# Moving one chunk's gate broadcast, two first states and four loads inside a fused mLSTM and MoE kernel

## The chip, the cores and the metric

The kernel runs on one core of a Trainium2 chip. The metric is the device time of one execution in microseconds (us). Three runs of the kernel before gave 401.60, 401.11 and 400.73 us, a median of 401.11 us. The execution whose trace is read here took 400.72 us; its instructions span 398.9 us, and 1.8 us lie around them. Durations come from that one execution, so a forecast is made as its 400.72 us plus or minus what the change does, and then set beside the median, which lies 0.39 us higher.

## The reference

Two stages are fused. The first is an mLSTM recurrence over 768 steps for 2 batches and 8 heads of width 40, with stabilised forget and input gates, an outer-product state, a normaliser and an output gate. The second is a mixture of four experts, each token weighted by given probabilities:

```python
C = f_stab[:, :, None, None] * C + i_stab[:, :, None, None] * np.einsum('bhd,bhe->bhde', vt, kt)
n = f_stab[:, :, None] * n + i_stab[:, :, None] * kt
y[:, :, t] = o * h_tilde / denom                      # denom = max(|n . q|, 1)
...
for e in range(E):
    h = np.maximum(x @ w1[e], 0.0)                    # 320 -> 1024
    out += p[:, e:e + 1] * (h @ w2[e])                # 1024 -> 320
```

## The kernel before, in words

The order of the work is written out by hand: every engine (TensorE or PE, VectorE or DVE, ScalarE or ACT, GpSimd or POOL) and SP's queue of transfers carries out its instructions in the order in which the program issues them. The recurrence is cut into 12 chunks of 128 steps; chunk n belongs to batch n % 2 and to place n // 2 in the sequence. Pairs of chunks share their loads (index j = n // 2).

What is done for a chunk:

- `load_qk(j)`, `load_vk(j)`, `load_o(j)` (L401 to L412) bring q and k, v and k, and the output gates. `load_o(j)` writes into two slices of the result tile `acc`; `gate_o(j)` (L414) turns them into sigmoids in place, on ACT.
- `spread(n)` (L421) copies a chunk's forget gates over all partitions with eight matmuls into two PSUM banks; this is done for chunks 0 to 3. From chunk 4 on, `load_f(n)` (L432) reads the same gates, broadcast, back from the scratch tensor `f_d`, 512 KB for each chunk. Chunk 4's go into a part of `acc` that is not used yet.
- `decay(n)` (L441) makes the decay matrix from them, in two scans on DVE; `scores(n)` (L470) is q times k on PE, `weigh(n)` (L478) multiplies the two on DVE.
- `values(n)` (L452) and `keys(n)` (L463) scale v and k on POOL. `state(n)` (L484) is the chunk's outer product on PE, added on DVE to what `carry(n)` (L506, POOL) scaled. For the first two chunks nothing is carried, and ACT copies the product.
- `inter(n)` (L515) reads the carried state on PE and scales it on ACT (`yb`), `intra(n)` (L534) does the part inside the chunk on PE, `norm(n)` (L543) adds the two, multiplies by the output gate and divides, on DVE (L551 to L558).
- `turn(n)` (L560) transposes the normalised chunk on PE into `px`, ACT copies the high part into `xst`, `turn_lo(n)` (L574) subtracts it on DVE for the low part. The experts' matmuls take both parts.

Gates of the chunks after the first are prepared together: `gate_p` (L326) puts start values into a PSUM bank, `gate_b` (L332) scans over them on DVE, `gate_last` (POOL), `gate_t` and `gate_l` (L348, L373) turn them to the layouts that the chunks want. The first expert's weights are split into a high part on ACT and a low part on POOL: `quarter_hi`, `quarter_lo` for w1, `split_w2` for w2 (L118 to L128).

PSUM has eight banks in four pools of two: `ps_h` (hidden products), `ps_o` (expert outputs, tag `po`), `ps_w` (tag `w`) and `ps_y` (tag `y`). A tile waits for the readers of the tile that had its bank before.

After a prologue written line by line (L581 to L715), a loop runs over chunks 2 to 11. In each it issues state(n), turn_lo(n - 1), inter(n + 1), intra(n), norm(n), scores(n + 1), then values, keys, weigh and carry of chunk n + 1, and then the pieces that `PLAN` (L38) lists for it: H (a hidden bank of the first expert), O (a part of its output), D (the first half of a later decay), T (turn). For chunk 2 the plan is "H03 D O00 T". From about 110 us on only the experts are left, four of them, 512 tokens at a time.

The transfers are all issued by SP. In the order of the program around the change: w1 of the first expert, qk(1), `pw` (the tokens' weights), the scratch write `f_d`, w2 of the first expert (`w2r`, 1,280 KB), vk(1) (640 KB), o(1) (320 KB), qk(2) (832 KB), vk(2) (640 KB), f(4) (512 KB), f(5), f(6), o(2), qk(3), vk(3).

Of the kernel before, what the change touches and what calls it, by code (L numbers as in the profile page):

```python
# [18 lines left out]
L = 128  # L19
# [16 lines left out]
NPE = 4  # L36
# [22 lines left out]
def tile_mlstm_moe(ctx, tc, gt, qk, vk, ot, dp, w1, w2, out):  # L59
# [33 lines left out]
    def copy(eng, dst, src):  # L93
        if eng is nc.scalar:
            eng.activation(dst, src, AF.Copy)
        else:
            eng.tensor_copy(dst, src)
# [147 lines left out]
    with ExitStack() as actx:  # L245
# [80 lines left out]
        def gate_p(c0, c1):  # L326

            n = (c1 - c0) * L
            bps[c0] = ps_w.tile([L, 512], F32, tag="w", name="bp")[0:BH, 0:n]
            nc.scalar.activation(bps[c0], bs[:, c0:c1].rearrange("p c t -> p (c t)"), AF.Copy)  # L330

        def gate_b(c0, c1):  # L332
# [72 lines left out]
        def load_vk(j, c=None):  # L405
            if j not in vks:
                vks[j] = a2.tile([L, 2, 2, H, D], F32, tag="vk", name="vk")
            c = slice(0, 2) if c is None else slice(c, c + 1)
            nc.sync.dma_start(vks[j][:, c], vk[j, :, c])
# [68 lines left out]
        def weigh(n):  # L478
            pms[n] = a1.tile([L, H, L], F32, tag=f"pm{n % 2}", name="pm")
            pm, dd = (t.rearrange("k (p r) t -> k r p t", r=2) for t in (pms[n], dds[n]))  # L480
            for r in range(2):
                nc.vector.tensor_mul(pm[:, r], ss[n][r], dd[:, r])  # L482

        def state(n, pool=ps_w, tag="w"):  # L484

            b, c, vv, kk = n % B, n // B, vvs[n], kp[n % 2]
            if c == NC - 1:
                return
            st = pool.tile([L, NP, L], F32, tag=tag, name="st")
            blocks = [(slice(64 * r, 64 * r + D), slice(DN * r, DN * r + DN)) for r in range(2)]  # L490
            for p in range(NP):
                for r, (q, q2) in enumerate(blocks):
                    h = 2 * p + r
                    nc.tensor.matmul(  # L494
                        st[q, p, q2], kk[:, h], vv[:, h, 0:D + 1], start=True, stop=True
                    )
            cout = cs[b]
            if c == 0:
                for q, q2 in blocks:
                    copy(nc.scalar, cout[q, :, q2], st[q, :, q2])  # L500
            else:
                cd = cds.pop(n)
                for q, q2 in blocks:
                    nc.vector.tensor_add(cout[q, :, q2], cd[q, :, q2], st[q, :, q2])

        def carry(n):  # L506
            b, c = n % B, n // B
# [77 lines left out]
        load_qk(0, 1)  # L585
        load_o(0)
        load_vk(0, 1)
        load_w1(0)
        load_w1(1)
        load_qk(1, 0)  # L590
        load_qk(1, 1)
        nc.sync.dma_start(pw, dp)
        make_identity(nc, ident)
        nc.gpsimd.memset(ib, 0.0)
        lasts[1] = gp.tile([L, B * NP, NC - 1], F32, name="last")
# [36 lines left out]
        for _ in range(3):  # L632
# [5 lines left out]
        gate_starts(1, NC, nc.gpsimd)  # L638
        gate_pair(1, 2, nc.gpsimd)
        values(1, LO)  # L640
        intra(0)
        nc.sync.dma_start(f_d, fs)
        w2r = raws.tile([L, NF, DM], F32, tag="raw", name="w2r")
        nc.sync.dma_start(w2r, w2[0])
        load_vk(1)
        load_o(1)
        load_qk(2)
        load_vk(2)
        load_f(NPE, acc[:, 8:12].rearrange("p c d -> p (c d)")[:, 0:H * L]
               .rearrange("p (h t) -> p h t", h=H))  # L650
        quarter_hi(0)
# [1 line left out]
        quarter_hi(1)  # L653
        norm(0)
        intra(1)
        turn(0)
        spread(2, ps_o, "po")
        norm(1)
        turn_lo(0)
        turn(1)  # L660
        keep_warm(256, ps_w, "w")
        gate_p(1, NC - 1)
        gate_p(NC - 1, NC)
        turn_lo(1)
        quarter_lo(1)
        quarter_hi(2)
        quarter_hi(3)
        keys(0)
        keys(1)
        quarter_lo(2)  # L670
        gate_b(1, NC - 1)
        gate_b(NC - 1, NC)
        gate_last(1, NC)
        quarter_lo(3)
        psum_e = const.tile([L, NCH, 1], F32, name="psum_e")
        nc.gpsimd.tensor_add(psum_e, pw[:, :, 0:1], pw[:, :, 1:2])
        for e in range(2, NE):
            nc.gpsimd.tensor_add(psum_e, psum_e, pw[:, :, e:e + 1])
        nc.gpsimd.tensor_scalar_add(psum_e, psum_e, 1e-9)
        first = work[0]  # L680
        first.products(0)
        turn_d(0, 2)
        nc.scalar.activation(ib[32:32 + BH, g1], gat[:, 0, g1], AF.Copy)
        decay(2)
        first.products(2)
        first.corners(0)
        first.relu(0)
        first.relu(2)
        scores(2)
        state(0, ps_y, "y")  # L690
        state(1, ps_y, "y")
        weigh(2)
        split_w2_hi(w2s, 0, 2, w2r)
        split_w2_hi(w2s, 2, 2, w2r)
        split_w2_lo(w2s, 0, 2, w2r, nc.gpsimd)
        spread(3, ps_o, "po")
        gate_t(1, NC)
        first.products(4)
        gate_l(1, NC)
        decay(3)  # L700
        values(2)
        keys(2)
        carry(2)
        split_w2_hi(w2s, 4, 2, w2r)
        split_w2_lo(w2s, 2, 2, w2r, nc.gpsimd)
        first.corners(4)
        first.relu(4)
        inter(2, ps_o, "po")
        gate_o(1)
        gctx.close()  # L710
        a0 = actx.enter_context(
            tc.tile_pool(name="a0", bufs=1, side="right", reuse_waits="tile")
        )
        load_f(NPE + 1)
        load_f(NPE + 2)  # L715

        def step(a):
            w, k = work[int(a[1])], int(a[2])
            if a[0] == "H":
# [5 lines left out]
        for n in range(2, NCH):  # L725
            j, cc = n // 2, n % 2
            plan = PLAN[n].split()
            nxt = n + 1 < NCH
            if cc == 0 and 2 < j + 1 < NG:
                load_qk(j + 1)  # L730
                load_vk(j + 1)
            if cc == 0:
                if j > 1:
                    gate_o(j)
                if j + 1 < NG:
                    load_o(j + 1)
            if n == NCH - 2:
                raw1 = load_w1e(1)
            state(n)
            if n - 1 in pxs:  # L740
                turn_lo(n - 1)
            if nxt:
                inter(n + 1)
            intra(n)
            norm(n)
            if nxt:
                scores(n + 1)
            for a in plan:
                if a[0] == "H":
                    work[int(a[1])].corners(int(a[2]) // 2 * 4)  # L750
                    break
            if nxt:
                values(n + 1)
                if n == 4:
                    split_w2_lo(w2s, 6, 2, w2r, nc.gpsimd)
                    nc.gpsimd.tensor_mul(pw, pw, psum_e.to_broadcast([L, NCH, NE]))
                if n > 2:
                    decay(n + 1, 1)
                if n > 3 and n + 3 < NCH:
                    load_f(n + 3)  # L760
                keys(n + 1)
                weigh(n + 1)
                carry(n + 1)
            if n == 2:
                split_w2_lo(w2s, 4, 2, w2r, nc.gpsimd)
                nc.vector.reciprocal(psum_e, psum_e)
            for a in plan:
                if a == "T":
                    turn(n, ps_w, "w")
                    turn_d(n, n + 1)  # L770
                elif a == "D":
                    decay(n + 2, 0)
                elif a == "L":
                    turn_lo(n)
                elif a == "S":
                    split_w2_hi(w2s, 6, 2, w2r)
                else:
                    step(a)
# [103 lines left out]
```

## Time and profile before

| | |
|---|---|
| median of three runs | 401.11 us |
| the profiled execution | 400.72 us |
| its span, first to last instruction | 398.9 us |
| PE busy | 393.3 us (99%) |
| DVE busy | 174.4 us (44%) |
| ACT busy | 128.1 us (32%) |
| POOL busy | 77.7 us (19%) |

Start and duration in a timeline are microseconds from the first instruction. "x8" says that eight instructions are merged. The bracket at the end of a line is the engine's idle time ahead of the line and what ended it; a line without one followed its predecessor at once. Matmuls overlap, so that a line of PE can start before the one ahead of it ends; the time that a group really takes is from its start to the next one's start.

### The profile page before, as it was taken

What the parts mean: (1) busy time and instruction counts of PE and PEld (TensorE: products, weight loads), DVE (VectorE), ACT (ScalarE), POOL (GpSimd) and SP (SyncE); (2) the same over time, 40 slices, a digit from 0 to 9 for tenths busy, and PEclk for the clock granted to TensorE, in tenths of its full rate; (3) what the DMA queues carried; (4) which work ended last, traced back from release to release, by engine and by line L of the source; (5) the groups of instructions that cost most, each with busy time, mean ns of one, the idle gap of its engine ahead of it and who ended that gap; (6) DMA issues with size and microseconds to landing.
All of it is one profiled execution on the core that took longest, in us unless ns stands there. A gap on an engine that the chain in (4) does not pass through costs nothing.

```text
span 398.9 us, 7170 instructions
## 1 busy us (share of the span) xinstructions
PE 393.3 (99%) x3054; PEld 357.4 (90%) x3054; DVE 174.4 (44%) x313; ACT 128.1 (32%) x309; POOL 77.7 (19%) x93
## 2 busy tenths in 40 slices
PE   9899999999999999999999999999999999999996
PEld 6799999999988988989989989889889889799896
DVE  8888989798624023133132152141241341331321
ACT  4876354455336332025021051071130320220310
POOL 4894622320007110007100010053000100000000
PEclk9999999999999999999999999999999999999999
DMA  6999529391000203000200031003000001000001
GB/s 159 316 307 283 157 82 250 89 284 83 2 2 12 121 18 139 2 0 19 114 2 0 2 106 52 2 1 133 0 2 0 2 0 49 18 16 35 17 18 49
DMA packets 15000, 29.34 MB, mean 74 GB/s; under 512 B 1000, under 2 KB 10760, under 8 KB 13656
## 3 DMA queue, kind: packets, MB, share of 16 engines
q1 hardware_dynamic: 14968, 28.88, 23.2%
q8 instruction: 24, 0.39, 0.4%
q14 instruction: 8, 0.07, 0.1%
HBM read 26.86 MB, written 2.02 MB: 72 GB/s over the span
## 4 chain that ended last, share of the span: by engine, by line
PE 96%; DMA 2%; DVE 1%; SPq 1%; issue 0%
PE ph L166 43%; PE po L226 43%; PE s L476 3%; PE y L538 2%; DMA qk<-in_qk 2%; PE y L523 2%; PE px L565 1%; PE st L494 1%; PE fb L426 0%; SPq L582 0%; DVE pm L482 0%; PE pit L356 0%; SPq L403 0%; DVE acc L236 0%; DVE xr L555 0%
## 5 line engine op out<-in xcount | busy, mean ns | idle before, releaser
L166 PE MATMUL ph<-xst,w1s 128*128 128x512 f32 (+3 forms) x840 | 174.9, 364 | 0.0
L226 PE MATMUL po<-w2s,h 128*128 128x320 f32 x1152 | 173.0, 309 | 0.0
L226 PEld LDWEIGHTS po<-w2s,h 128*128 128x128 f32 x1152 | 169.9, 188 | 1.2
L166 PEld LDWEIGHTS ph<-xst,w1s 128*128 128x128 f32 (+1 forms) x840 | 140.9, 188 | 28.3 <-issue 4.2
L209 ACT ACTIVATE h<-ph 128x512 fp32r<-128x512 f32 x96 | 57.3, 598 | 194.3 <-PE ph L166 194.3
L210 DVE SCALAR_TENSOR_TENSOR h<-ph,h 128x512 fp32r<-128x512 f32 x96 | 66.2, 690 | 102.1 <-ACT h L209 101.5
L236 DVE SCALAR_TENSOR_TENSOR acc<-po,pw,acc 128x320 f32<-128x320 f32 x36 | 19.8, 551 | 99.9 <-PE po L226 99.9
L109 POOL TENSOR_TENSOR w1s<-raw,w1s 128x512 fp32r<-128x512 f32 (+1 forms) x24 | 23.6, 1023 | 96.6 <-ACT w1s L106 96.6
L109 POOL TENSOR_TENSOR w2s<-raw,w2s 128x640 fp32r<-128x640 f32 x6 | 9.5, 1576 | 98.2 <-ACT w2s L106 98.2
L445 DVE TENSOR_TENSOR_SCAN dd<-fb,id 128x512 f32<-128x512 f32 x22 | 26.7, 1231 | 0.0
L530 ACT ACTIVATE yb<-y,ibT 128x41 f32<-128x41 f32 x80 | 16.0, 322 | 0.8 <-PE y L523 0.8
L166 PE MATMUL ph<-xd,w1s 64*128 64x512 f32 (+1 forms) x56 | 15.9, 392 | 0.0
L482 DVE TENSOR_TENSOR pm<-s,dd 128x512 f32<-128x512 f32 x24 | 15.4, 684 | 1.0
L476 PE MATMUL s<-qk 64*128 64x128 f32 (+1 forms) x192 | 15.2, 284 | 0.6 <-DMA qk<-in_qk 0.6
L476 PEld LDWEIGHTS s<-qk 64*128 64x128 f32 (+1 forms) x192 | 13.0, 187 | 1.8 <-DVE dd L445 1.0
L465 POOL TENSOR_TENSOR kp<-vk,dd 128x320 f32<-128x320 f32 x10 | 7.4, 740 | 35.3 <-DVE dd L445 35.3
L106 ACT ACTIVATE w2s<-raw 128x640 fp32r<-128x640 f32 x12 | 8.8, 733 | 16.4 <-DMA raw<-in_w 16.4
L538 PE MATMUL y<-vp,pm 128*64 128x41 f32 x384 | 13.2, 229 | 0.2 <-POOL vp L459 0.2
L538 PEld LDWEIGHTS y<-vp,pm 128*64 128x64 f32 x384 | 12.3, 138 | 0.6 <-POOL vp L459 0.3
L459 POOL TENSOR_TENSOR vp<-vk,ibT 128x320 f32<-128x320 f32 x12 | 10.6, 882 | 3.7 <-PE y L538 3.5
L234 ACT ACTIVATE acc<-po,pw 128x320 f32<-128x320 f32 x12 | 6.3, 529 | 15.1 <-PE po L226 15.1
L106 ACT ACTIVATE w1s<-raw 128x512 fp32r<-128x512 f32 (+1 forms) x24 | 11.2, 517 | 0.0
(86 smaller groups left out, 178.5 us busy)
## 6 DMA issues: line engine op xcount, KB each, us to landing
raw<-in_w SPq DMA_DIRECT2D x3, 1536.0 KB, 7.9
raw<-in_w SPq DMA_DIRECT2D x3, 1280.0 KB, 5.4
fb<-f_d SPq DMA_DIRECT2D x7, 512.0 KB, 8.0
qk<-in_qk SPq DMA_DIRECT2D x4, 832.0 KB
vk<-in_vk SPq DMA_DIRECT2D x5, 640.0 KB, 10.0
acc<-in_ot SPq DMA_DIRECT2D x6, 320.0 KB, 11.3
out<-acc SPq DMA_DIRECT2D x12, 160.0 KB, 1.8
qk<-in_qk SPq DMA_DIRECT2D x4, 416.0 KB
```

The costliest lines, as they stand in the source:

```text
L106: nc.scalar.activation(hi, raw, AF.Copy)
L109: eng.tensor_sub(lo, raw, hi.bitcast(F32))
L166: nc.tensor.matmul(self.banks[i][:, f % self.nf, :], self.w1s[r, wi, f * L:(f + 1) * L], x[r, self.t0:self.t0 + self.n], start=(i not in s ...
L209: nc.scalar.activation(hh, ph, AF.Relu)
L210: nc.vector.scalar_tensor_tensor(out=hl, in0=ph, scalar=0.0, in1=hh.bitcast(F32), op0=ALU.max, op1=ALU.subtract)
L226: nc.tensor.matmul(po, self.hs[f][a][:, sl], ws[:, b, f, :], start=(first and i == 0), stop=(last and i == len(ks) - 1),)
L236: nc.vector.scalar_tensor_tensor(out=acc[:, i, :], in0=po, scalar=pw[:, i, e:e + 1], in1=acc[:, i, :], op0=ALU.mult, op1=ALU.add,)
L445: nc.vector.tensor_tensor_scan(out=dds[n][:, 4 * i:4 * i + 4].rearrange("p h t -> p (h t)"), data0=fbs[n][i].rearrange("p h t -> p (h t)") ...
L476: nc.tensor.matmul(ss[n][r][:, p, :], kg[q, p], qg[q, p], start=True, stop=True)
L482: nc.vector.tensor_mul(pm[:, r], ss[n][r], dd[:, r])
L530: nc.scalar.activation(yb[:, h], y1[:, h // 2, d:d + DN], AF.Copy, scale=ibT[:, c, i:i + 1])
L538: nc.tensor.matmul(y[t, h, 0:D + 1], pms[n][:, h, t], vvs[n][:, h, 0:D + 1], start=True, stop=True,)
```

## The change

Spread of chunk 3 is issued ahead of chunk 1's turn, into `ps_w`, and spread of chunk 2 ahead of chunk 0's turn. The first states of both batches are made in one bank by a new function, followed at once by `gate_t`, ahead of chunk 2's scores, which move to `ps_o`. Chunk 3's decay is issued in two halves around chunk 2's weigh. The splits of w2 move down, keys(2) goes ahead of values(2), `psum_e` (sums of the tokens' weights) goes up to before `intra(0)`, `gate_last` goes down behind `quarter_lo(3)`, and `gate_p` uses `ps_y`. Of the transfers, `pw` goes ahead of w1, vk(1) ahead of w2r, o(1) behind qk(2) and vk(2), and f(5), f(6) behind o(2).

```diff
         def gate_p(c0, c1):
-            bps[c0] = ps_w.tile([L, 512], F32, tag="w", name="bp")[0:BH, 0:n]
+            bps[c0] = ps_y.tile([L, 512], F32, tag="y", name="bp")[0:BH, 0:n]
...
+        def state_0():
+            st = ps_y.tile([L, B, NP, 64], F32, tag="y", name="st")
+            blocks = [(slice(64 * r, 64 * r + D), slice(DN * r, DN * r + DN)) for r in range(2)]
+            for n in range(B):
+                for p in range(NP):
+                    for r, (q, q2) in enumerate(blocks):
+                        h = 2 * p + r
+                        nc.tensor.matmul(
+                            st[q, n, p, 0:DN], kp[n][:, h], vvs[n][:, h, 0:D + 1],
+                            start=True, stop=True,
+                        )
+            for n in range(B):
+                for q, q2 in blocks:
+                    copy(nc.scalar, cs[n][q, :, q2], st[q, n, :, 0:DN])
...
         load_vk(0, 1)
+        nc.sync.dma_start(pw, dp)
         load_w1(0)
         load_w1(1)
         load_qk(1, 0)
         load_qk(1, 1)
-        nc.sync.dma_start(pw, dp)
...
         values(1, LO)
+        psum_e = const.tile([L, NCH, 1], F32, name="psum_e")
+        nc.gpsimd.tensor_add(psum_e, pw[:, :, 0:1], pw[:, :, 1:2])
+        for e in range(2, NE):
+            nc.gpsimd.tensor_add(psum_e, psum_e, pw[:, :, e:e + 1])
+        nc.gpsimd.tensor_scalar_add(psum_e, psum_e, 1e-9)
         intra(0)
         nc.sync.dma_start(f_d, fs)
+        load_vk(1)
         w2r = raws.tile([L, NF, DM], F32, tag="raw", name="w2r")
         nc.sync.dma_start(w2r, w2[0])
-        load_vk(1)
-        load_o(1)
         load_qk(2)
         load_vk(2)
+        load_o(1)
         load_f(NPE, acc[:, 8:12].rearrange("p c d -> p (c d)")[:, 0:H * L]
...
         norm(0)
         intra(1)
+        spread(2, ps_o, "po")
         turn(0)
-        spread(2, ps_o, "po")
+        spread(3, ps_w, "w")
         norm(1)
         turn_lo(0)
         turn(1)
-        keep_warm(256, ps_w, "w")
+        keep_warm(256)
         gate_p(1, NC - 1)
-        gate_p(NC - 1, NC)
         turn_lo(1)
         quarter_lo(1)
         quarter_hi(2)
+        gate_p(NC - 1, NC)
         quarter_hi(3)
...
         gate_b(NC - 1, NC)
+        decay(2)
+        quarter_lo(3)
         gate_last(1, NC)
-        quarter_lo(3)
-        psum_e = const.tile([L, NCH, 1], F32, name="psum_e")
...
-        decay(2)
         first.products(2)
         first.corners(0)
         first.relu(0)
         first.relu(2)
-        scores(2)
-        state(0, ps_y, "y")
-        state(1, ps_y, "y")
+        state_0()
+        gate_t(1, NC)
+        scores(2, ps_o, "po")
+        decay(3, 0)
         weigh(2)
-        split_w2_hi(w2s, 0, 2, w2r)
-        split_w2_hi(w2s, 2, 2, w2r)
-        split_w2_lo(w2s, 0, 2, w2r, nc.gpsimd)
-        spread(3, ps_o, "po")
-        gate_t(1, NC)
+        decay(3, 1)
         first.products(4)
         gate_l(1, NC)
-        decay(3)
+        keys(2)
         values(2)
-        keys(2)
         carry(2)
-        split_w2_hi(w2s, 4, 2, w2r)
-        split_w2_lo(w2s, 2, 2, w2r, nc.gpsimd)
+        split_w2_hi(w2s, 0, 2, w2r)
+        split_w2_lo(w2s, 0, 2, w2r, nc.gpsimd)
         first.corners(4)
         first.relu(4)
         inter(2, ps_o, "po")
+        split_w2(w2s, 2, 2, w2r, nc.gpsimd)
         gate_o(1)
...
-        load_f(NPE + 1)
-        load_f(NPE + 2)
...
                 if j + 1 < NG:
                     load_o(j + 1)
+                if n == 2:
+                    load_f(NPE + 1)
+                    load_f(NPE + 2)
...
             if n == 2:
-                split_w2_lo(w2s, 4, 2, w2r, nc.gpsimd)
+                split_w2(w2s, 4, 2, w2r, nc.gpsimd)
                 nc.vector.reciprocal(psum_e, psum_e)
```

## Rows read from the trace of the kernel before

**Rows 1.** The page: PE's busy time, and the granted TensorE clock in 40 slices.

```profile
PE 393.3 (99%) x3054; PEld 357.4 (90%) x3054; DVE 174.4 (44%) x313; ACT 128.1 (32%) x309; POOL 77.7 (19%) x93
...
PEclk9999999999999999999999999999999999999999
```

**Rows 2.** Timeline of PE, 13 to 28 us (start, duration, engine, line, operation).

```profile
13.43 1.14 PE L538 MATMUL y<-vp,pm 128*64 128x41 f32 x32 [0.16 <-POOL vp L459]
15.19 0.52 PE L565 MATMUL px<-ident,xr 128*128 128x128 f32 x3 [0.62 <-DVE xr L558]
15.46 1.09 PE L426 MATMUL fb<-fr,sel 128*128 128x128 f32 x8
16.64 0.52 PE L565 MATMUL px<-ident,xr 128*128 128x128 f32 x3
...
17.63 4.20 PE L166 MATMUL ph<-xst,w1s 128*128 128x256 f32 x29
...
23.52 1.11 PE L426 MATMUL fb<-fr,sel 128*128 128x128 f32 x8
24.56 0.79 PE L356 MATMUL pit<-ident,ib 128*64 128x48 f32 x20
```

**Rows 3.** Timeline of PE, 30 to 39 us.

```profile
30.39 1.16 PE L476 MATMUL s<-qk 64*128 64x128 f32 x16
...
35.02 0.49 PE L565 MATMUL px<-ident,xr 128*128 128x128 f32 x3
...
37.38 1.50 PE L476 MATMUL s<-qk 64*128 64x128 f32 x16
```

**Rows 4.** Timeline of DVE, 31 to 45 us.

```profile
31.00 0.51 DVE L551 TENSOR_TENSOR y<-y,yb 128x328 f32<-128x328 f32 x1 [0.89 <-ACT acc L416]
...
32.60 0.49 DVE L558 TENSOR_TENSOR xr<-xr,y 128x320 f32<-128x320 f32 x1
...
35.14 1.22 DVE L445 TENSOR_TENSOR_SCAN dd<-acc,id 128x512 f32<-128x512 f32 x1 [0.18 <-DMA acc<-f_d]
...
37.39 0.28 DVE L577 TENSOR_TENSOR xst<-px,xst 64x128 fp32r<-64x128 f32 x1
...
42.10 1.37 DVE L445 TENSOR_TENSOR_SCAN dd<-fb,id 128x512 f32<-128x512 f32 x1
...
44.61 0.28 DVE L577 TENSOR_TENSOR xst<-px,xst 64x128 fp32r<-64x128 f32 x1
```

**Rows 5.** Timeline of ACT, 27 to 31 us.

```profile
27.60 0.73 ACT L106 ACTIVATE w2s<-w2r 128x640 fp32r<-128x640 f32 x1
...
28.71 1.60 ACT L530 ACTIVATE yb<-y,ibT 128x41 f32<-128x41 f32 x8
30.13 0.80 ACT L416 ACTIVATE acc<-acc 128x640 f32<-128x640 f32 x1
```

**Rows 6.** Timeline of SP's transfers: issues of o(1) and qk(2).

```profile
15.79 0.51 SPq L412 DMA_DIRECT2D acc<-in_ot  x1
17.36 0.33 SPq L403 DMA_DIRECT2D qk<-in_qk  x1
```

**Rows 7.** Tile `acc`, SP alone, 15.7 to 16.4 us: o(1), issue to landing.

```profile
DMA to landing us min/median/max: 12.4/12.4/12.4
```

**Rows 8.** Windows: busy time of the engines, then granted clock, DMA's share, GB/s.

```profile
22.00:24.00 2.00, 2.00 (x52) 1.83 (x49) 1.61 (x4) 1.72 (x5) 1.92 (x4) 1.00 0.97 407
...
28.00:30.00 2.00, 2.00 (x72) 1.90 (x66) 1.14 (x3) 2.00 (x10) 2.00 (x3) 1.00 0.83 191
...
33.50:35.10 1.60, 1.60 (x13) 1.59 (x12) 1.46 (x4) 0.60 (x1) 1.40 (x2) 1.00 0.99 294
```

**Rows 9.** Timeline of POOL, 14 to 25 us: first low part of w1, first and last of `psum_e`.

```profile
14.24 1.28 POOL L109 TENSOR_TENSOR w1s<-wa,w1s 128x512 fp32r<-128x512 f32 x1 [0.87 <-ACT w1s L106]
...
23.59 0.20 POOL L676 TENSOR_TENSOR psum_e<-pw 128x12 f32<-128x12 f32 x1
...
24.47 0.24 POOL L679 TENSOR_SCALAR psum_e<-psum_e 128x12 f32<-128x12 f32 x1
```

More of the change, by code (lines that the diff above doesn't have):

```diff
@@ L496, in state @@
                     )
[L497 to L504, printed above, removed]
+            cout, cd = cs[b], cds.pop(n)
+            for q, q2 in blocks:
+                nc.vector.tensor_add(cout[q, :, q2], cd[q, :, q2], st[q, :, q2])
         def carry(n):
@@ L672, in tile_mlstm_moe @@
         gate_b(NC - 1, NC)
+        decay(2)
+        quarter_lo(3)
         gate_last(1, NC)
-        quarter_lo(3)
-        psum_e = const.tile([L, NCH, 1], F32, name="psum_e")
[L676 to L679, printed above, removed]
         first = work[0]
```

## The prediction

> **What bounds the kernel now.** I read the page first: PE is busy for 393.3 of the 398.9 us and its granted clock is full in every slice [rows 1]. So whatever lengthens PE's queue, or leaves PE without work, is paid at the end, and nothing after 110 us can make up for it. Next PE's timeline, for the places where it waits or is filled. At the front there is one hole: intra(1) ends at 14.57 (13.43 + 1.14), and the transpose of chunk 0 starts only at 15.19, 0.62 us later, when norm(0) is done; from the first expert's products at 17.63 on, no line has idle time ahead of it [rows 2]. That does not mean that PE waits for nobody. Scores take 1.16 us for chunk 3, at 30.39, but 1.50 us for chunk 4, at 37.38 [rows 3]: a wait of some 0.34 us lies inside the line. DVE's timeline says for what: turn_lo(2), which frees the PSUM bank that these scores want, ends at 37.67 (37.39 + 0.28), and turn_lo(3) ends at 44.89 in the same way, right where scores(5) come [rows 4]. So between 31 and 45 us DVE runs level with PE, and its queue is the second thing to watch. I followed it back: L551, the start of norm(2), sits idle for 0.89 us until gate_o(1) is over, and decay(4) waits 0.18 us for the broadcast f(4) [rows 4]. Gate_o(1) itself runs on ACT right behind yb(2), from 30.13 to 30.93 [rows 5]. Last the transfers: o(1), which gate_o(1) reads, was issued at 15.79 and landed 12.4 us later, at 28.2 [rows 6, 7], 1.9 us before its reader. All that time the DMA engines are 0.83 to 0.99 busy, at between 191 and 407 GB/s [rows 8]: a transfer lands when all that was queued ahead of it is through.
>
> **The change, part by part.**
>
> *Spreads at the front (a gain, first term).* The spread of chunk 3 takes 1.04 us of PE's full queue now (23.52 to 24.56, where the next line starts) [rows 2]. It moves ahead of turn(1), and spread(2) ahead of turn(0). Spread(2) fills the hole from 14.57: at about 0.95 us it ends at 15.5, so turn(0) comes 0.3 us later than its 15.19; spread(3) then runs from about 15.9 to 16.9, and turn(1) starts at 16.9 instead of 16.64 [rows 2]. ACT's copy of turn(1) releases the products, so these start some 0.25 us late. Net on PE: 1.04 - 0.25 = 0.8 us earlier from there on. That is all that PE can win, since it has no other hole.
>
> *State_0, gate_t, scores(2), decay(3) halves, banks (nothing).* The matmuls are the same in number and shape; only their order changes. Their cover is DVE: decay(2) is over well before scores(2) want its bank, and decay(3) halves stand where DVE has room before L551's wait of 0.89 us [rows 4]. If that cover failed, scores(2) would wait for a scan half, 1.2 us at most.
>
> *Psum_e on POOL (nothing).* Four small operations take 1.12 us (23.59 to 24.47 + 0.24). POOL now has 0.87 us idle ahead of the first low part of w1, at 14.24 [rows 9]; placed there they push it by about 0.25 us, to an end at some 16 us, and the products that read it start at 17.63 or later. The later low parts of w1 inherit 0.25 us; vk(2), which waits on SP's queue for keys(1) on POOL, does too, and with it o(1) and f(4) that stand behind it now; all three are issued some 10 us before the engines reach them, as o(1)'s 12.4 us show [rows 7], so the queue never runs dry.
>
> *Splits of w2, gate_last, gate_p (nothing).* Three splits of w2, 0.73 us each, stood on ACT ahead of gate_o(1); two stand there now, one of them between yb(2) and gate_o(1) [rows 5]. ACT waits for gate_l on PE ahead of them, so PE's gain of 0.8 and this split of 0.73 cancel: without its data's delay gate_o(1) would come at about 30.1, as now.
>
> *pw, vk(1), w2r (nothing).* Pw is 24 KB. Vk(1) lands earlier, w2r later by vk(1)'s 640 KB, 2.2 us at 294 GB/s [rows 8]; its first split was moved down by about as much.
>
> *o(1) behind qk(2) and vk(2) (the loss, second term).* 832 + 640 KB = 1.51 MB now go ahead of it. What is queued ahead of f(4) stays the same, only reordered, so f(4) still lands at about 35.1 [rows 4], and o(1) lands one f(4) earlier. F(4) is 0.524 MB; at 294 GB/s, the rate of the 1.6 us before it landed [rows 8], 1.8 us: 33.3. The other way round gives the same: 28.2 [rows 6, 7] plus 1.51 MB at 294 GB/s, 5.1 us, is 33.3. The ends: 407 and 191 GB/s [rows 8] put o(1) at 33.8 and 32.4 when counted back from f(4), and 407 from the front at 31.9. I take 33.3, since the rate of 294 is that of the same transfers' own stretch.
> Queued behind gate_o(1) on ACT are yb(3), values(3)'s column, a split of w2 and a relu; waiting for it on DVE is norm(2), and behind that weigh(3), decay(4), state(3)'s sum and turn_lo(2). Gate_o(1) would run from 33.35 to 34.1, L551 start at 34.2 instead of 31.00: 3.2 us late. The wait of 0.18 us for f(4) disappears in that, so turn_lo(2) ends 3.2 - 0.18 = 3.0 us late, at 40.7 instead of 37.67, and scores(4) with it. On PE, turn(2) already waits for norm(2), which ends 2.1 us after L551 starts (32.60 + 0.49 - 31.00) [rows 4], so at 36.3; PE would have been there at 35.02 - 0.8 = 34.2 [rows 3]. The front's 0.8 us are swallowed by that wait, so they are not taken off a second time. From scores(4) on PE has again no hole, and DVE no late work beyond what it has now: the 3.0 us stay to the end.
> The bounds: with o(1) at 31.9 the loss is 1.6 us, at 33.8 it is 3.5 us. If L551, which needs yb(2), runs ahead of the sigmoid and only the next step waits, its 0.51 us come off, and 2.5 us are left.
>
> *f(5), f(6) behind o(2) (nothing).* O(2) is 320 KB, 1.1 us at 294 GB/s. F(5) would land near 35.1 + 1.1 + 1.8 = 38.0; its reader is the scan at 42.10 [rows 4], 3 us later with the shift. F(6) follows by another 1.8 us and is read a chunk later.
>
> **The sum.** 400.72 + 3.0 = 403.7 us for an execution like the profiled one; the median stands 0.39 us above it, so 404.1 us.
>
> **The rivals.**
>
> *No change: o(1) lands in time.* If the engines moved the queue fast enough for o(1) to land by 30.1, gate_o(1) would run when it does now. PE would still arrive 0.8 us early and wait at scores(4), because L551 and f(4) hold DVE as now: 401.0 us. For it speaks that o(1) has 1.9 us to spare now. Against it, 1.51 MB in 1.9 us would be 790 GB/s, and the fastest window shows 407 [rows 8].
> *A smaller loss: the queue runs at its best.* If qk(2) and vk(2) moved at 407 GB/s, the fastest window [rows 8], o(1) would land at 31.9 and 1.6 us be lost: 402.7 us. Against it, the window in which they do move, from 28 us on, shows 191 GB/s with the engines 0.83 busy: they are slow by themselves.
> The Trainium skill, "DMA: Bandwidth & Descriptors", Specifications, speaks for this rival: about 27 GiB/s for each of 16 engines, some 464 GB/s; by it 1.51 MB are an estimate of 3.3 us, o(1) at 31.5, and the loss 1.2 us. The window's 191 GB/s does not agree with it, and I go by the window.
>
> *Faster: the filled hole is kept.* Its place is PE at 14.57, its price the 0.8 us worked out above: 400.3 us. It decides only if f(4) lands before 34.3 and gate_o(1) is over before 30.2, so that DVE too is 0.8 us early at turn_lo(2). Nothing ahead of f(4) is removed, and the sigmoid needs its data; I see nothing in the rows that moves either.
>
> *Slower still: the clock.* PE would stand still for 2.1 us before turn(2) (34.2 to 36.3) and, 2.36 us of work later (35.02 to 37.38), for 2.0 us more before scores(4) [rows 3]. In this trace the clock stayed full through a hole of 0.62 us [rows 1, 2]; nothing shows one of 2 us. If it fell to 1.2 GHz behind such a hole, each microsecond of matmuls at that level would cost another half; 2 to 4 us of them make 405 to 406 us.
>
> **How the numbers follow.** A measurement of this kernel can tell about 0.2%, 0.8 us, from no change. The forecast, slower by a late o(1), has 0.74; the smaller loss 0.08; slower still by the clock 0.04; no change 0.10; faster 0.04. So slower 0.86, same 0.10, faster 0.04. The likeliest case gives 404.1 us. The bounds of its loss, 1.6 and 3.5 us, give 402.7 to 404.6, and half the spread of the three runs (0.87 us) on either side makes it 402.2 to 405.0. That takes in the smaller loss and leaves out the other three, 0.18.
>
> **What would show it.** Right: o(1) landing near 33.3 in the trace after; L551 of chunk 2 with an idle time of 3 us or more, ended by ACT's sigmoid (L416); ACT idle ahead of that sigmoid until a DMA; PE idle ahead of turn(2), with DVE named, and ahead of or inside scores(4); products of the first expert at about 17.9, spread(3) at about 16. Wrong: o(1) landed by 30, or the sigmoid still at 30 us. If f(4) lands much earlier than 35, the count of the queue's bytes is wrong; if scores(2) or inter(2) show idle time, the banks are; if PE's granted clock falls under 1.0, the clock case holds.

## The result and the profile after

The kernel after takes 403.58 us, the median of 20 executions from 402.09 to 405.95; the kernel before takes 401.09 us on the same chip (20 executions, 400.56 to 404.14). The ratio is 1.0057, with a 95% interval of 1.0042 to 1.0072: slower by 2.5 us, inside the range and close to the forecast of 404.1 us. The profiled execution of after took 402.09 us and is the fastest of its 20, so its trace shows a loss of 1.37 us (402.09 - 400.72), and the median one is larger.

The timeline of PE in the kernel after (columns as before: start, duration, engine, line, operation, and in the bracket the idle time ahead and what ended it), to be read beside [rows 2, 3]:

```profile
14.71 1.11 PE L426 MATMUL fb<-fr,sel 128*128 128x128 f32 x8
15.66 0.52 PE L576 MATMUL px<-ident,xr 128*128 128x128 f32 x3
15.93 1.09 PE L426 MATMUL fb<-fr,sel 128*128 128x128 f32 x8
16.87 0.52 PE L576 MATMUL px<-ident,xr 128*128 128x128 f32 x3
...
17.86 4.19 PE L166 MATMUL ph<-xst,w1s 128*128 128x256 f32 x29
...
29.54 0.48 PE L549 MATMUL y<-vp,pm 128*64 128x41 f32 x9 [0.21 <-issue]
...
34.97 0.55 PE L576 MATMUL px<-ident,xr 128*128 128x128 f32 x3 [0.23 <-DVE pm L482]
...
38.42 0.46 PE L476 MATMUL s<-qk 64*128 64x128 f32 x2 [0.75 <-DVE cs L515]
39.08 1.16 PE L476 MATMUL s<-qk 40*128 40x128 f32 x14 [0.20 <-DVE xst L588]
40.16 3.78 PE L226 MATMUL po<-w2s,h 128*128 128x320 f32 x24
```

The front is as drawn: the hole of 0.62 us ahead of the first transpose is gone, spread(3) starts at 15.93, and the products start at 17.86, 0.23 us later than before. Further on the idle times stand where there were none: 0.21 us inside intra(2), for which the profile names no releaser ("issue"), 0.23 us ahead of turn(2), 0.75 and 0.20 us at scores(4). From turn(2) on the name in the brackets is always DVE (at turn(2) it is L482, the multiply of weigh(3) that follows norm(2)). Its timeline in the same kernel, beside [rows 4] (L562 to L569 are norm, before L551 to L558; L588 is the second half of turn_lo, before L577):

```profile
30.14 0.51 DVE L562 TENSOR_TENSOR y<-y,yb 128x328 f32<-128x328 f32 x1 [0.78 <-PE y L549]
30.68 0.17 DVE L563 TENSOR_SCALAR nq<-y 128x8 f32<-128x8 f32 x1
32.84 0.49 DVE L566 TENSOR_TENSOR xr<-y,acc 128x320 f32<-128x320 f32 x1 [1.99 <-ACT acc L416]
...
36.13 1.58 DVE L445 TENSOR_TENSOR_SCAN dd<-acc,id 128x512 f32<-128x512 f32 x1
...
38.74 0.28 DVE L588 TENSOR_TENSOR xst<-px,xst 64x128 fp32r<-64x128 f32 x1
```

Only the multiply with the output gate, L566, waits for ACT's sigmoid; the sum L562 and the step after it ran ahead of it, as soon as PE was done. In the trace of before the same multiply, L555, started at 31.62:

```profile
31.62 0.48 DVE L555 TENSOR_TENSOR xr<-y,acc 128x320 f32<-128x320 f32 x1
```

Further down, the scan of decay(4) takes 1.58 us where it took 1.22, and turn_lo(2) ends at 39.02 (38.74 + 0.28) instead of 37.67. ACT's timeline says what the sigmoid waited for, beside [rows 5]:

```profile
27.95 1.59 ACT L541 ACTIVATE yb<-y,ibT 128x41 f32<-128x41 f32 x8
29.37 0.80 ACT L106 ACTIVATE w2s<-w2r 128x640 fp32r<-128x640 f32 x1
32.06 0.74 ACT L416 ACTIVATE acc<-acc 128x640 f32<-128x640 f32 x1 [1.89 <-DMA acc<-in_ot]
```

It waited for o(1), the transfer that was moved. SP's timeline gives its issue, and the tile view of `acc` (SP alone, 20.3 to 20.7 us) its time to landing, beside [rows 6, 7]; the window is that in which it moves, beside [rows 8]:

```profile
20.46 0.42 SPq L412 DMA_DIRECT2D acc<-in_ot  x1
```

```profile
DMA to landing us min/median/max: 11.6/11.6/11.6
```

```profile
30.00:32.00 2.00, 2.00 (x25) 1.88 (x25) 0.67 (x2) 0.17 (x1) 1.75 (x2) 1.00 1.06 367
```

So o(1) landed at about 32.06, 20.46 + 11.6, where it was there at 28.2 before. Last POOL, of which the prediction expected nothing in this stretch:

```profile
35.08 1.55 POOL L109 TENSOR_TENSOR w2s<-w2r,w2s 128x640 fp32r<-128x640 f32 x1 [1.21 <-ACT w2s L106]
36.59 1.64 POOL L459 TENSOR_TENSOR vp<-vk,ibT 128x320 f32<-128x320 f32 x1
```

The third low part of w2 now runs from 35.08 to 36.63 and lies across the start of the scan. The next operation, values(4), takes 1.64 us; the same operation a chunk earlier takes 0.73.

**One number tells the rest.** In both traces the time of the whole execution is the end of turn_lo(2) plus the same amount: 400.72 - 37.67 = 363.05 before, 402.09 - 39.02 = 363.07 after. What comes after turn_lo(2) takes as long in both. The loss of 1.37 us is therefore made of what DVE did up to there: the gate's multiply 1.22 us later (32.84 against 31.62), less the wait of 0.18 us for f(4), which is gone, plus 0.36 us of a longer scan; that is 1.40 us, and the operations between give back 0.05. All experiments below are read by these three: the start of the multiply, the duration of the scan, the end of turn_lo(2).

### The profile page after: what moved, and what is told of

It is laid out like the page before. It is cut to its first block, busy times and chain, and to the rows that moved or that the text cites. A ratio compares the mean times of both kernels' runs of the same rounds, so it can differ in the third digit from the quotient of the medians.

```text
span 400.3 us, 7167 instructions
## 1 busy us (share of the span) xinstructions
PE 394.5 (99%) x3054; PEld 358.0 (89%) x3054; DVE 174.8 (44%) x313; ACT 127.5 (32%) x309; POOL 78.7 (20%) x93
## 4 chain that ended last, share of the span: by engine, by line
PE 89%; DMA 3%; POOL 3%; DVE 2%; issue 1%; ACT 0%; SPq 0%; POOLq 0%; DVEq 0%
PE po L226 42%; PE ph L166 41%; DMA acc<-in_ot 3%; PE s L476 2%; PE y L549 2%; PE y L534 1%; POOL w1s L109 1%; PE px L576 1%; PE st L510 1%; DMA gat<-in_gt 1%; DVE mb L304 0%; POOL fs L312 0%; POOL vp L459 0%; POOL fs L313 0%; DVE pm L482 0%
## 5 line engine op out<-in xcount | busy, mean ns | idle before, releaser
L166 PE MATMUL ph<-xd,w1s 64*128 64x512 f32 (+1 forms) x56 | 15.9, 392 | 0.0
L482 DVE TENSOR_TENSOR pm<-s,dd 128x512 f32<-128x512 f32 x24 | 15.3, 681 | 0.8
L465 POOL TENSOR_TENSOR kp<-vk,dd 128x320 f32<-128x320 f32 x10 | 7.4, 742 | 33.3 <-DVE dd L445 33.3
L459 POOL TENSOR_TENSOR vp<-vk,ibT 128x320 f32<-128x320 f32 x12 | 11.5, 956 | 3.9 <-PE y L549 3.4
```

The lines of the kernel that those rows point to most:

```text
L166: nc.tensor.matmul(self.banks[i][:, f % self.nf, :], self.w1s[r, wi, f * L:(f + 1) * L], x[r, self.t0:self.t0 + self.n], start=(i not in s ...
```

## Experiments

The theory: o(1) lands late, and through sigmoid, norm(2) and DVE's queue it sets scores(4); the front's gain is real but swallowed. The rivals: the loss comes from the parts that were costed at nothing (the moved splits of w2, f(5) and f(6), the spreads), or from the clock. Every kernel ran beside the kernel before, which had a median of 401.35 us in the first group (the first four), 401.11 in the second (the next four) and 401.31 in the third.

### e1_o1_early: the kernel after with o(1) issued early again

```diff
         nc.sync.dma_start(w2r, w2[0])
+        load_o(1)
         load_qk(2)
         load_vk(2)
-        load_o(1)
```

> The changed kernel with o(1) issued ahead of qk(2), vk(2) as before; all else of the change kept. Theory A (the late o(1) holds the sigmoid, norm(2) and all behind it on DVE): o(1) lands near 27 to 28 us, ACT's idle time ahead of gate_o(1) goes, norm(2)'s product with the gate starts near 31 instead of 32.8, and the time falls from 403.6 to 400.4 to 401.2 us. Rival B (banks, order of scores and states): stays at 403 to 404. Rival C (f(5), f(6) issued later): stays at 403 to 404.

Measured: 402.11 us (400.71 to 404.81, 12 executions), ratio 1.0023 (1.0002 to 1.0044). That is above the 400.4 to 401.2 us expected; by the medians 1.5 of the 2.5 us come back. The six executions with a mean granted clock of 0.999 or more have a median of 400.85 us; the other six, at 0.995 to 0.996, one of 403.47. The profiled execution, 402.27 us, is one of the latter. DVE and POOL in its trace:

```profile
30.65 0.49 DVE L566 TENSOR_TENSOR xr<-y,acc 128x320 f32<-128x320 f32 x1 [0.43 <-ACT acc L416]
...
34.04 2.29 DVE L445 TENSOR_TENSOR_SCAN dd<-acc,id 128x512 f32<-128x512 f32 x1
...
37.36 0.28 DVE L588 TENSOR_TENSOR xst<-px,xst 64x128 fp32r<-64x128 f32 x1
```

```profile
33.67 1.55 POOL L109 TENSOR_TENSOR w2s<-w2r,w2s 128x640 fp32r<-128x640 f32 x1
35.18 1.67 POOL L459 TENSOR_TENSOR vp<-vk,ibT 128x320 f32<-128x320 f32 x1
```

With o(1) early the sigmoid is on time, and the multiply is 0.97 us earlier than before (30.65 against 31.62): what the front has won arrives here. But the scan takes 2.29 us instead of 1.22, and turn_lo(2) ends at 37.64, level with the 37.67 of before. So the wait for o(1), and what it cost, is gone; and there is a second cost, the split on POOL, which was costed at nothing. Then PE's timeline and its granted clock:

```profile
37.03 0.46 PE L476 MATMUL s<-qk 64*128 64x128 f32 x2 [0.65 <-DVE cs L515]
37.70 1.16 PE L476 MATMUL s<-qk 40*128 40x128 f32 x14 [0.21 <-DVE xst L588]
38.78 5.32 PE L226 MATMUL po<-w2s,h 128*128 128x320 f32 x24
```

```profile
37.00:39.00 2.00, 1.76 (x17) 1.48 (x18) 1.88 (x7) 0.84 (x3) 0.00 (x0) 1.00 1.09 255
39.00:40.00 1.00, 1.00 (x6) 1.00 (x6) 0.97 (x3) 0.00 (x0) 0.00 (x0) 0.57 0.96 199
40.00:41.00 1.00, 1.00 (x5) 1.00 (x5) 0.90 (x2) 0.00 (x0) 0.15 (x1) 0.50 0.88 207
```

The 24 matmuls take 5.32 us against 3.78 after: the clock column falls to 0.50, the lower level of 1.2 GHz, from 39 to 42.5 us, behind two short waits of PE. That is 1.54 us, and the time agrees: 402.27 - 37.64 = 364.63, 1.57 more than 363.06.

### e2_before_o1_late: the kernel before, with o(1) alone moved back

```diff
-        load_o(1)
         load_qk(2)
         load_vk(2)
+        load_o(1)
```

> The kernel before with one edit: o(1) issued behind qk(2) and vk(2). Theory A: o(1) lands at 32 to 33.5 us, the sigmoid and norm(2) wait for it, scores(4) start 2 to 3 us late, time 403.3 to 404.3 us. Rivals B and C: 401.1 us, since banks, order and f(5), f(6) are those of before.

Measured: 403.51 us (402.56 to 405.25, 6 executions), ratio 1.0058 (1.0037 to 1.0079), which is the ratio of the whole change. DVE in its trace, with the line numbers of before:

```profile
32.88 0.51 DVE L551 TENSOR_TENSOR y<-y,yb 128x328 f32<-128x328 f32 x1 [1.85 <-PE y L538]
...
34.80 0.49 DVE L555 TENSOR_TENSOR xr<-y,acc 128x320 f32<-128x320 f32 x1 [1.22 <-ACT acc L416]
...
38.07 1.21 DVE L445 TENSOR_TENSOR_SCAN dd<-acc,id 128x512 f32<-128x512 f32 x1
```

The multiply is 3.18 us late, the scan is its old 1.21 us since POOL's split ends before it, and turn_lo(2) ends at 40.58; the profiled 403.66 us are 363.08 more. By the times, one moved line makes the loss by itself. And L551 starts at 32.88 while the sigmoid, by ACT's timeline, starts only at 34.03: L551 does not need it. The bracket of [rows 4] named the sigmoid because it happened to end last, at 30.93:

```profile
34.03 0.74 ACT L416 ACTIVATE acc<-acc 128x640 f32<-128x640 f32 x1 [3.52 <-DMA acc<-in_ot]
```

This trace does not give the whole 3.18 us to o(1), though. The stream of transfers was late in this execution ahead of the moved line too: w2r landed at 25.2 us against 24.3 before, and values(2) on POOL waited 0.69 us for vk(1). PE then waited for keys(2), which follow values(2):

```profile
29.69 0.51 PE L494 MATMUL st<-vp,kp 128*40 128x41 f32 x16 [0.97 <-POOL kp L465]
```

That put scores(3) at 32.29 instead of 30.39 and L551 at 32.88, and would have put the multiply near 33.6 with o(1) on time; the sigmoid adds 1.22 us to it. That the moved line makes the loss rests on the six times, of which the lowest, 402.56, is above 22 of the 23 executions of the kernel before in this group.

### e3_o1_behind_f4: the kernel after, with o(1) one place later still

```diff
-        load_o(1)
         load_f(NPE, acc[:, 8:12].rearrange("p c d -> p (c d)")[:, 0:H * L]
...
+        load_o(1)
```

> The changed kernel with o(1) moved one place further back, behind f(4), 0.5 MB more ahead of it. Theory A: it lands 1.5 to 1.9 us later than in the changed kernel and the whole loss grows by as much: 405.1 to 405.6 us. Rivals B and C: no more than 0.3 us from 403.6.

Measured: 405.09 us (403.58 to 406.64, 6 executions), ratio 1.0094 (1.0073 to 1.0115). The dose answers: a later transfer, a later end (405.1 to 405.6 us were expected). In its trace (403.58 us) the sigmoid starts at 33.55, 1.49 us later than in the kernel after, and the multiply follows:

```profile
34.32 0.49 DVE L566 TENSOR_TENSOR xr<-y,acc 128x320 f32<-128x320 f32 x1 [4.08 <-ACT acc L416]
```

The scan takes 1.57 us, turn_lo(2) ends at 40.50. PE waits 2.30 us ahead of turn(2), and the windows show the clock behind that:

```profile
34.00:36.40 2.40, 0.14 (x1) 0.00 (x0) 1.98 (x6) 2.40 (x12) 0.00 (x0) 1.00 0.98 281
36.40:38.00 1.60, 1.56 (x21) 1.18 (x23) 1.60 (x4) 1.17 (x5) 1.43 (x1) 0.51 0.90 232
```

The half clock comes while PE would have to wait for DVE at scores(4) anyway, so in this execution it costs nothing: 403.58 - 40.50 is 363.08 again.

### e4_o1_early_f4_ahead: o(1) early and f(4) ahead of vk(2)

```diff
         nc.sync.dma_start(w2r, w2[0])
+        load_o(1)
         load_qk(2)
-        load_vk(2)
-        load_o(1)
         load_f(NPE, ...)
+        load_vk(2)
```

> The changed kernel with o(1) ahead of qk(2), and f(4) ahead of vk(2) too, so that the second transfer that DVE waits for is early as well. If the filled hole at the front is worth what the prediction said and only the two transfers took it away: about 400.3 us, 0.8 under before, with scores(4) near 36.9 us on PE. If DVE holds PE anyway: 401.1. If vk(2), now about 1.8 us later, is wanted early by POOL: over 401.5.

Measured: 400.73 us (400.64 to 402.93, 11 executions), ratio 0.9995 (0.9984 to 1.0006): level with before, and not the gain of 0.8 us that was to be tested. DVE and POOL in its trace (400.64 us):

```profile
33.98 2.33 DVE L445 TENSOR_TENSOR_SCAN dd<-acc,id 128x512 f32<-128x512 f32 x1
```

```profile
33.68 1.55 POOL L109 TENSOR_TENSOR w2s<-w2r,w2s 128x640 fp32r<-128x640 f32 x1
```

The scan's gates are in time here, and still it takes 2.33 us. It ends at 36.31, 1.08 us after the split's end at 35.23. The same difference stands in the other traces with such an overlap: 37.71 - 36.63 = 1.08 in the kernel after, 36.33 - 35.22 = 1.11 in e1, and 1.08 in e3 and e8. And values(4), behind the split, ends only after the scan in all five (in e4 it also waits 0.78 us for vk(2), which now stands behind f(4)). The two engines do not slow each other in proportion; one waits for the other to end.

### e5_splits_apart and e9_third_split_later: the split taken out of the scan's way

e5 is e4 with each split of w2 one place earlier, so that the third is through before the scan:

```diff
         first.products(4)
+        split_w2_hi(w2s, 0, 2, w2r)
...
-        carry(2)
-        split_w2_hi(w2s, 0, 2, w2r)
         split_w2_lo(w2s, 0, 2, w2r, nc.gpsimd)
+        carry(2)
+        split_w2_hi(w2s, 2, 2, w2r)
+        split_w2_lo(w2s, 2, 2, w2r, nc.gpsimd)
...
-        split_w2(w2s, 2, 2, w2r, nc.gpsimd)
+        split_w2_hi(w2s, 4, 2, w2r)
...
-                split_w2(w2s, 4, 2, w2r, nc.gpsimd)
+                split_w2_lo(w2s, 4, 2, w2r, nc.gpsimd)
```

> The fourth experiment (o(1) early, f(4) ahead of vk(2)) with the splits of w2 each one place earlier on ACT and POOL, so that POOL's third one is over when DVE scans chunk 4's first half. Theory D (that scan, 2.3 us instead of 1.2 us there, waits for POOL's operation because the two exclude one another): the scan takes 1.2 to 1.4 us, turn_lo(2) ends near 36.6 instead of 37.6, scores(4) start a microsecond earlier, 399.7 to 400.2 us. Rival (the scan is long for another reason, such as its operand from the late transfer): it still takes over 2 us and the time stays at 400.7.

Measured: 400.48 us (399.58 to 401.83, 12 executions), ratio 0.9991 (0.9976 to 1.0006). The executions fall into two lots of six, 399.58 to 400.03 and 400.92 to 401.83. Only the lower lot lies near the 399.7 to 400.2 us expected; the median does not. The trace is of the lower lot (399.86 us): scan 1.36 us, turn_lo(2) at 36.80. DVE and POOL in it:

```profile
34.13 1.36 DVE L445 TENSOR_TENSOR_SCAN dd<-acc,id 128x512 f32<-128x512 f32 x1
```

```profile
33.69 0.72 POOL L459 TENSOR_TENSOR vp<-vk,ibT 128x320 f32<-128x320 f32 x1 [0.73 <-DMA vk<-in_vk]
```

The last 0.15 us of the scan are the same thing on a small scale: values(4), late for vk(2), ends at 34.41, and the scan ends 1.08 us after it, at 35.49.

e9 is e4 with the third split later, its high part at the end of chunk 2's iteration and its low part on POOL behind values(4):

```diff
+                if n == 3:
+                    split_w2_lo(w2s, 4, 2, w2r, nc.gpsimd)
                 if n == 4:
...
             if n == 2:
-                split_w2(w2s, 4, 2, w2r, nc.gpsimd)
                 nc.vector.reciprocal(psum_e, psum_e)
...
+            if n == 2:
+                split_w2_hi(w2s, 4, 2, w2r)
```

> The fourth experiment (o(1) early, f(4) ahead of vk(2)) with one split of w2 (its third quarter) moved down: its high part on ACT behind turn(2), its low part on POOL behind values(4), after DVE's scan of chunk 4 instead of in front of it. Unlike the fifth experiment nothing is moved up towards w2r's landing. Theory D (scan and POOL exclude one another; o(1), f(4) and this split are all that held the gain): the scan takes 1.2 to 1.4 us, scores(4) start near 36.7 us, 399.6 to 400.2 us with no second group of runs near 401.7. Rival (the fifth experiment's slow half had another cause than w2r's landing): two groups again, median over 400.5.

Measured: 400.13 us (399.52 to 402.44, 9 executions), ratio 0.9977 (0.9960 to 0.9994). DVE and POOL in its trace (399.58 us):

```profile
30.77 0.49 DVE L566 TENSOR_TENSOR xr<-y,acc 128x320 f32<-128x320 f32 x1 [0.44 <-ACT acc L416]
...
34.03 1.21 DVE L445 TENSOR_TENSOR_SCAN dd<-acc,id 128x512 f32<-128x512 f32 x1
...
36.27 0.28 DVE L588 TENSOR_TENSOR xst<-px,xst 64x128 fp32r<-64x128 f32 x1
```

```profile
35.06 0.72 POOL L459 TENSOR_TENSOR vp<-vk,ibT 128x320 f32<-128x320 f32 x1 [1.23 <-PE st L510]
```

The scan is back at 1.21 us and values(4) at 0.72, with the multiply and the data as in e4. Turn_lo(2) ends at 36.55, 1.12 us earlier than before, and the time is 1.14 us less (399.58 against 400.72). So the scan's extra length came from the overlap with the split, which is all that was moved. This version is 0.23% faster than the kernel before, with an interval that just leaves out no change; three of its nine executions are at 400.5 to 400.6 us, and one with a lower mean clock is at 402.44.

### e6, e8, e10: the spreads put back

The same edit on e5, on the kernel after and on e9:

```diff
         intra(1)
-        spread(2, ps_o, "po")
         turn(0)
-        spread(3, ps_w, "w")
+        spread(2, ps_o, "po")
...
         decay(3, 0)
         weigh(2)
+        spread(3, ps_w, "w")
         decay(3, 1)
```

> The fifth experiment with the spreads of chunks 2 and 3 back where they were before (2 behind turn(0), 3 in PE's full queue behind scores(2)); nothing else. If the filled hole is worth 0.8 us on PE once no transfer and no split holds DVE: 0.6 to 0.9 us slower than the fifth experiment. If DVE alone sets the pace from chunk 2 on: no difference.

> The changed kernel with the spreads of chunks 2 and 3 back where they were before, o(1) still late. The prediction said that the front's 0.8 us are swallowed by the wait for o(1): then no more than 0.3 us from the changed kernel's 403.6. If the front's gain and the wait add up instead: 404.4.

> The ninth experiment with the spreads of chunks 2 and 3 back where they were before. The prediction's first term alone, with nothing to swallow it: 0.6 to 0.9 us slower than the ninth, 400.4 to 400.9 us. If the spreads are worth nothing on PE: no difference.

Measured: e6 400.67 us (400.41 to 401.57, 12 executions), ratio 0.9991 (0.9980 to 1.0002); e8 403.72 us (402.71 to 406.33, 6), ratio 1.0081 (1.0054 to 1.0109); e10 400.56 us (400.36 to 402.15, 11), ratio 0.9984 (0.9975 to 0.9993). On the kernel after, the spreads are worth 0.14 us by the medians (403.72 against 403.58) and 0.24% by the ratios, with intervals that overlap: no gain is shown there, as predicted, though six executions cannot exclude one. On e9, with o(1) and f(4) early and the split away, they are worth 0.43 us by the medians and 0.84 by the fastest executions (400.36 against 399.52), again with intervals that overlap. On e5 the medians differ by 0.19 only, within e5's two lots, where 0.6 to 0.9 was expected. The traces are clearer. From the start of the first expert's products to inter(2) PE takes 10.00 us in e6, e8 and e10 (17.69 to 27.69 in e6), and 9.19, 9.11 and 9.12 us in e5, the kernel after and e9: 0.81 to 0.89 us.

e8 has another use: it is a second trace of the transfers' new order. There the sigmoid started when o(1) landed, at 33.32:

```profile
33.32 0.74 ACT L416 ACTIVATE acc<-acc 128x640 f32<-128x640 f32 x1 [2.13 <-DMA acc<-in_ot]
```

The multiply started at 34.09, the scan took 1.58 us again, and the time was 403.33 us. O(1)'s landing differs by 1.3 us between two executions with the same order of transfers.

### e7_f56_back and e11_f4_behind_vk2: where the broadcasts stand

e7 is e5 with f(5), f(6) issued ahead of o(2) again; e11 is e9 with vk(2) ahead of f(4), the order of the kernel after:

```diff
+        load_f(NPE + 1)
+        load_f(NPE + 2)
...
-                if n == 2:
-                    load_f(NPE + 1)
-                    load_f(NPE + 2)
```

> The fifth experiment with f(5) and f(6) issued ahead of o(2), as before the change. The prediction costed this edit at nothing: within 0.2 us of the fifth experiment. Rival C (their place in the queue matters): over 0.5 us apart.

```diff
         load_qk(2)
+        load_vk(2)
         load_f(NPE, ...)
-        load_vk(2)
```

> The ninth experiment with f(4) back behind vk(2), 0.64 MB later. The prediction said that f(4) near 35 us alone holds DVE and swallows the front's gain: then 0.5 to 1.0 us slower than the ninth, 400.4 to 401.0 us, with idle time of DVE ahead of the scan of chunk 4, ended by the transfer. If f(4) is in time there too: within 0.2 us.

Measured: e7 400.83 us (399.69 to 403.98, 12 executions), ratio 0.9994 (0.9975 to 1.0013), 0.35 us from e5 by the medians, where 0.2 or less was expected, and no difference that can be told. Its trace (400.67 us, between e5's two lots) has two waits that e5's does not have. ACT's first split waits 1.50 us for w2r, its low part holds POOL, and the carry behind it is 0.34 us late for DVE. And PE stands still for 0.92 us inside intra(2), with no releaser named, for which L562 waits last:

```profile
30.69 0.51 DVE L562 TENSOR_TENSOR y<-y,yb 128x328 f32<-128x328 f32 x1 [0.69 <-PE y L549]
```

No trace of e5's upper lot exists, so what makes it stays open.

e11: 401.06 us (399.88 to 405.19, 12), ratio 1.0013 (0.9989 to 1.0036), 0.93 us over e9 and just above the 400.4 to 401.0 expected. Its trace has the multiply at 30.65, but DVE idle for 1.53 us ahead of the scan, until f(4) landed at about 35.5:

```profile
35.53 1.23 DVE L445 TENSOR_TENSOR_SCAN dd<-acc,id 128x512 f32<-128x512 f32 x1 [1.53 <-DMA acc<-f_d]
```

So f(4) is the second transfer that can hold DVE: with the whole front 0.8 us early, its place matters.

## Why the prediction was right, and which of its steps failed

**The late o(1)** was right as a chain: ACT idle until a DMA, DVE idle until the sigmoid, PE idle until DVE, and nothing given back later. e1 takes the wait away (what its trace still loses is the scan and the clock), e2 makes the loss with one moved line, e3 makes it larger. The landing was sized at 33.3 with ends of 31.9 and 33.8; it was about 32.06 in the trace of after and 33.3 in that of e8. The step was sound, but the landing has no single value, and the rate is not fixed: from 28 to 30 and from 30 to 32 us the windows read 258 and 367 GB/s after, and 221 and 320 in e8 with the same order, where before reads 191 for the first [rows 8]. The same bytes, in another order, were through at 35.1 us before [rows 4], at 33.55 in e3 (o(1) last) and at 35.5 in e11 (f(4) last). The rival with the faster queue, o(1) at 31.9, is close to what the profiled execution shows.

**"L551 start at 34.2"** failed, and the bound beside it held. The step took the bracket of [rows 4], L551 idle for 0.89 us until the sigmoid, for a need; the bracket only names who ended last. L551 (L562 now) adds `yb` to PE's products and reads no gate, as the code of norm says, and in e2 it ran 1.15 us before the sigmoid began. So only the multiply waited. In both traces of the old code L551 starts 0.6 us after scores(3) begin (31.00 - 30.39, 32.88 - 32.29), so it may have waited for PE in both; that is not shown. From landing to multiply it took 0.78 us (32.06 to 32.84) where the forecast's way takes 1.5 (33.3 to 34.2, and 0.62 for L551 and L552). That is 0.7 us less loss. In e8, with o(1) at 33.3 as forecast, the multiply came 2.47 us late (34.09 - 31.62), where the bound has 2.5 us of loss.

**"Splits of w2 (nothing)"** failed. The step counted them on ACT, where they cancel the front's gain, and did not follow the low part to POOL, where it came to lie across decay(4)'s scan: 0.36 us in the kernel after, some 1.1 us in e1 and e4, as much as the front wins. The trace of before had a hint: the scan of 1.37 us at 42.10 [rows 4] starts while POOL's carry runs (its line in the timeline of POOL before is below) and ends 1.09 us after it, and values(5) behind it take 1.67 us instead of 0.73:

```profile
41.64 0.74 POOL L510 TENSOR_TENSOR cd<-cs,bl 104x328 f32<-104x328 f32 x1
42.33 1.67 POOL L459 TENSOR_TENSOR vp<-vk,ibT 128x320 f32<-128x320 f32 x1
```

The Trainium skill states the rule in "SBUF — State Buffer", section "SBUF: two separate sides": VectorE and GpSimd share a pair of ports under an exclusive lock, which a VectorE operation with two SBUF inputs takes against a GpSimd operation that reads SBUF; whoever comes second is blocked until the other ends. The traces agree, by the 1.08 to 1.11 us from POOL's end to the scan's end in six of them (after, e1, e3, e4, e5, e8), about a scan's own length; and in e7, where the scan starts first (34.88), it keeps its 1.21 us and values(4), started at 35.02, take 1.59. A scan over gates in PSUM is not held. In the kernel after, this one starts beside keys(2) on POOL:

```profile
24.11 1.21 DVE L445 TENSOR_TENSOR_SCAN dd<-fb,id 128x512 f32<-128x512 f32 x1
```

```profile
24.09 0.73 POOL L465 TENSOR_TENSOR kp<-vk,dd 128x320 f32<-128x320 f32 x1
```

Both keep their length, and so does values(2) at 24.96 (0.72 us).

**The front** was right in being swallowed, and its size came out within 0.1 us, in part because two errors offset each other. Spread(3) at 15.93 and the products at 17.86 meet the 15.9 and 17.88 forecast by luck: in that execution intra(1) itself started 0.22 us late (13.65 against 13.43 [rows 2]). From intra(1) to the products it is 4.20 us before and 4.21 in the kernel after and in e9. In before and after alike the second transpose starts 0.14 us after norm(1)'s last operation on DVE, so the moved spreads delay nothing, and the 0.25 us that the forecast took off are not there. On the other side a spread takes 0.95 us of the full queue (e6, 24.36 to 25.31) rather than 1.04. So 0.81 to 0.89 us are measured where 0.8 was forecast. From the products to scores(3) it is 12.76 us before (17.63 to 30.39 [rows 2, 3]) and 12.53 in e6, with the spreads back: these 0.23 us come from the other edits, which were not tried apart. In e9 it is 11.65, in the profiled execution of after 12.10, because of the stop inside intra(2), whose cause is open.

**The sum.** In the profiled execution turn_lo(2) came 1.35 us late instead of 3.0: 1.24 less for the earlier landing (33.3 - 32.06), 0.72 less for L562 and its handover, 0.36 more for the scan; that leaves 1.40, and 0.05 is the give-back above. For an execution with o(1) at 33.3 the last two give 404.1 - 0.72 + 0.36 = 403.7 us, and the median is 403.58. The trace of e8, with o(1) at 33.3, fits: without the 0.39 us between the profiled execution and the median the sum is 403.35, and it took 403.33. That the median execution of the kernel after has o(1) near 33.3 is argued from this, not traced. So the forecast was too high by 0.72 us for one step and too low by 0.36 for the other, and that they offset each other by half is luck.

**The clock** rival was priced for waits of 2 us. PE waited less in the kernel after (0.20 to 0.75 us at a time), and in the profiled execution the clock stayed full. But four of its 20 executions had a mean clock of 0.991 to 0.996, and their median is 404.4 us against 403.4 of the other 16. So the rival fits a tail of the executions, not the main case.

**Of the parts costed at nothing,** banks, gate_t, psum_e and gate_last show no wait in the trace after, nor do f(5) and f(6), whose place e7 tried without a difference that can be told. The others were not tried one by one.

## What to carry to other kernels

Before a transfer is moved behind others, find its reader and the queue behind that reader: the reader here was one short sigmoid on an engine with time to spare, and it cost 2.5 us of a full PE. A gain at the front of a queue is worth only as much as the tightest later meeting point lets through; find that point (here the end of turn_lo(2)) and list everything that ends just ahead of it, each of which has to move too. A bracket names what ended last, so check in the code that the operation reads it. And where VectorE is that point, look at what GpSimd does beside its operations on two SBUF tiles: an operation that is free on its own engine can cost the other one all that is left of its length.

## What was not expected of the hardware

The lower clock came behind short waits of PE, and not always. In e1 the waits were 0.65 and 0.21 us and the clock fell to 0.50; in e4 they were 0.62 and 0.20 us at the same place of the same work, and the clock stayed at 1.00 from 37 to 43 us. In the trace of e10 (402.15 us) it is at or near 0.50 between 16 and 19 us, behind a hole of 0.63 us; one of 0.62 us at the same place left it full in the kernel before [rows 1, 2]. What decides it is open. A fall behind turn_lo(2) cost 1.6 us (e1 and e11: 364.63 us of the time lie behind it, against 363.02 to 363.08 in the eleven other traces). Executions with a mean clock of 0.998 or less were 6 of 12 in e1, 5 of 6 in e3, 5 of 12 in e11, 2 of 6 in e8, 4 of 20 after, 1 of 9 in e9 and none of 6 in e2.

The other surprise is how far the stream of transfers moves between executions: o(1) landed at 32.06 us in the kernel after and at 33.3 in e8, under the same order of the queue. One profiled execution can then show the right mechanism with a size that is not the median's, and here it was the fastest of 20.
